# Half of a decode layer's result leaves through ScalarE, with its residual added in PSUM, and one store in place of two

## The chip, the cores and the metric

The kernel runs on one core of a Trainium2 chip. The metric is device time in microseconds (us) from start to end of one execution; lower is better. Of the kernel before, three runs are known: 189.81, 189.96 and 190.07 us, median 189.96. Engines are named as in the profile: PE (TensorE, matrix products), PEld (its weight loads), DVE (VectorE), ACT (ScalarE), POOL (GpSimd), SP (SyncE, which here only issues transfers and waits).

## What is computed

One token (a row `x` of 512 numbers) goes through an attention block with a cached context, and then through a small mixer and MLP block:

```python
def _A_ref(x, k_cache, v_cache, wq, wo):      # 32 query heads, 8 key/value heads, 16384 keys of 128
    q = (x @ wq) per head
    p = softmax(q k^T * 128**-0.5)
    return (p v over all heads) @ wo
def _B_ref(x, w1, w2, w3, w4):
    h  = gelu(layernorm(x) @ w1)
    hs = shifted quarters of h @ w2           # a shift over a sequence of one: all zero
    x1 = x + hs                               # so x1 = x, and w1, w2 are not needed
    return x1 + gelu(layernorm(x1) @ w3) @ w4
h  = x + _A_ref(layernorm(x), ...)
h2 = h + _B_ref(layernorm(h), ...)            # 512 bfloat16 numbers: the result
```

The caches are 2 x 32 MB of bfloat16, so nearly all bytes are keys and values. The result is the sum of a residual (`h` plus its normalised self, since `_B_ref` adds its input) and the product with `w4`.

## The kernel before, in words

**Stages.** The query projection comes first, then a loop over 4 pairs of key/value heads, and then a tail: the product with `wo`, the layer norm, the product with `w3`, gelu, the product with `w4`, the addition of the residual, the store. All large loads are issued by SP on one queue, in the order in which they are used: `wq`, keys, values, ..., `wo` (2 pieces), `w3`, `w4` (3 pieces, cut at groups 8 and 13 of 14, `W4`).

**How the code is recorded.** A helper class `Program` records operations with the keys that they read (`r`), write (`w`) and the PSUM banks that they use (`bank`). `op` (line 50) turns these into waits. For a bank it makes an operation wait for the last user of that bank on every other engine (lines 66 to 69), whatever part of the bank either touches. `_tensor` (line 159) folds PE's part of the loop over the pairs into a real loop on the engine, with registers: `r` ("seen") holds the DVE count to wait for, `rl` ("landed") the count of a POOL semaphore that tells which pair's values have landed. POOL's operation there is a `nop` that waits for the transfer and raises the semaphore by `worth`, which is 1.

**The tail as far as the change touches it.** `h_ps` is PSUM bank 6. The row of 512 is kept as 4 blocks of 128 columns; block `o` stands on partitions 32o to 32o+31, every one of them the same. `hT` and `hr` hold `h`; `st[1]` (`s`) holds its statistics, a column for each: `s[:, 6:7]` is an inverse root that POOL works out (`inverse_root(1, 0, pool, pool)`, line 787), `s[:, 13:14]` that plus one (line 788). ACT makes `xsum`, the residual on all 128 partitions, from `xs`, a per-partition scale `s[:, 13:14]` and a per-partition bias `s[:, 12:13]` (line 799). Gelu runs in two halves on ACT (line 791), each turned over by DVE into `hcol` (line 795). The product with `w4` (line 805) has 14 groups (`m`) of 4 matmuls (`o`), each with weights `hcol[:, m, :]` and 128 columns of `w4`; the groups from 7 on need the second half of `hcol`, those from 8 on the second piece of `w4`, group 13 the third. DVE adds `h_ps` and `xsum` into `fin` (line 810). Partitions 31 and 32 of `fin` hold blocks 0 and 1, partitions 95 and 96 blocks 2 and 3; SP stores the first two rows and ACT the other two (line 817), and SP waits for both (line 820).

Of the kernel before, what the change touches and what calls it, by code (L numbers as in the profile page):

```python
# [24 lines left out]
class Program:  # L25
# [133 lines left out]
    def _tensor(self):  # L159
        nc, eng, ops = self.nc, self.nc.tensor, self.ops["PE"]  # L160
        inside = [n for n, o in enumerate(ops) if o.at is not None]
        lo, hi = inside[0], inside[-1] + 1
        at = {o.at: o for o in ops[lo:hi]}
        assert len(at) == len(inside) == hi - lo
        loop = [o for o in ops[lo:hi] if o.at[0] != "query"]
        pairs = 1 + max(o.at[1] for o in loop)
        last = pairs - 1

        def places(kind, *rest):
            return sorted(a for a in at if a[0] == kind and a[1:1 + len(rest)] == rest)  # L170
# [3 lines left out]
        def least(o):  # L174
            return max((d.val - d.worth + 1 for d in o.deps if d.eng == "DVE" and not d.dma), default=0)
# [6 lines left out]
        parts = 1 + max(a[2] for a in places("value", last))  # L182
        step = least(at[("key", 2, 0, 0, 0)]) - least(at[("key", 1, 0, 0, 0)])
# [7 lines left out]
        first = waits["key", last, 0, 0, 0] - 1  # L191
        keys = {("key", last, y, c, 0): first + 1 + pieces * y + c for y in range(2) for c in range(pieces)}
        rest = {(a[0], a[-1]): v for a, v in waits.items() if a[0] in ("middle", "rest")}
# [5 lines left out]
        for o in loop:  # L199
            a = o.at  # L200
            v = waits.get((a[0], last, *a[2:]))
# [6 lines left out]
        told = {}  # L208
# [4 lines left out]
            for d in ds:  # L213
                told.setdefault(o.at[1:3], set()).add((d.sem, d.val - d.worth + 1, d.val))
        told = {k: max(v, key=lambda x: x[2]) for k, v in told.items()}
        sem, v0, _ = told[0, 0]
        for (j, x), (_, lo_v, hi_v) in told.items():
            assert lo_v <= v0 + parts * j + x <= hi_v
        assert v0 > 0 and first - step * last > 0

        r, rl, ry, rq, rk = (eng.alloc_register(n) for n in ("seen", "landed", "half", "query", "piece"))
        hint = eng.mark_branch_hint_location()
        eng.reg_mov(r, first + 1 - step * last)
        eng.reg_mov(rl, v0 - 1)
        seen = {}
        self._run(eng, ops[:lo], seen)
        query = [at[a] for a in places("query", 0)]
# [51 lines left out]

        nc.switch_bb("pe_middle", parent=None)  # L280
        now, again = first + 1 + 2 * pieces, 0
        eng.reg_add(rl, rl, 1)

        def straight(kind):
            nonlocal now, again
# [18 lines left out]
                nc.switch_bb(f"pe_ready{again}", parent=None)  # L304

        straight("middle")
        for x in range(parts):
            if x:
                eng.reg_add(rl, rl, 1)
            eng.wait_ge(sem, rl)  # L310
            for a in places("value", 1, x):
                self._issue(eng, at[a])
        straight("rest")
        assert now == final
        eng.reg_add(r, r, first + 1 - (final - step))
        eng.reg_add(ry, ry, -2 * 512 - again)
        eng.br_lt(rl, v0 - 1 + parts * pairs, "pe_piece", "pe_after")

        nc.switch_bb("pe_after", parent=None)
        seen[id(vector)] = final  # L320
# [16 lines left out]
            done = more + ops[more].many  # L337
        self._run(eng, ops[done:on], seen)

        eng.br_lt(rl, 0, "pe_piece", "pe_on").branch_hint(hint)  # L340
        nc.switch_bb("pe_on", parent=None)
        self._run(eng, ops[on + 1:], seen)

# [10 lines left out]
NHC = FM // 128  # L354
WO = ((0, 20), (20, 32))
VP = 1
W3 = ((0, 4),)
W4 = ((0, 8), (8, 13), (13, 14))
PAIRS = HKV // 2
# [12 lines left out]
def bass_sequential_preLN__gqa_block_cached__mixer_s_mlp__decode_kernel(  # L372
# [13 lines left out]
    with ExitStack() as ctx:  # L386
        sb = lambda name, shape, dt: ctx.enter_context(nc.sbuf_tensor(name, shape, dt))
        ps = lambda name, shape, dt: ctx.enter_context(nc.psum_tensor(name, shape, dt))
        P = Program(nc, ctx)
# [33 lines left out]
        bias = sb("bias", [128, 1], FP32)  # L423
# [11 lines left out]
        rs = [sb(f"rs{i}", [128, 2], FP32) for i in range(2)]  # L435
        hc = sb("hc", [128, NCH, 32], BF16)
        xs = sb("xs", [128, 128], FP32)
        xsum = sb("xsum", [128, 128], FP32)
        hg = sb("hg", [128, FQ], BF16)
        hT = sb("hT", [128, NCH, 32], FP32)  # L440
        hcol = sb("hcol", [128, NHC, 32], BF16)
        fin = sb("fin", [128, 128], BF16)
        kb_all = sb("kb", [128, 256 * DH], BF16)
        kb = [kb_all[:, i * 128 * DH:(i + 1) * 128 * DH] for i in range(2)]
        vb = sb("vb", [128, 256 * DH], BF16)
# [24 lines left out]
        def load_values(j):  # L470
            n = 256 // VP * DH
            if j < PAIRS - 1:
                load("v", vb[:, :], pair_rows(A_v_cache, j), ("v", 0),
                     also=[("v", x) for x in range(1, VP)] + [("landed", x) for x in range(VP)])
                P.op("POOL", lambda e: e.nop(), r=[("v", 0)], w=[("landed", x) for x in range(VP)], worth=VP,
                     own="v")
                return
            for x in range(VP):
                load(f"v{x}", vb[:, x * n:(x + 1) * n], pair_rows(A_v_cache, j)[:, x * n:(x + 1) * n], ("v", x),
                     also=[("landed", x)])  # L480
            for x in range(VP):
                P.op("POOL", lambda e: e.nop(), r=[("v", x)], w=[("landed", x)], own="v")  # L482


        def dve(fn, r=(), w=(), bank=()):
            return P.op("DVE", fn, r, w, bank)

        def act(fn, r=(), w=(), bank=()):
            return P.op("ACT", fn, r, w, bank)
# [57 lines left out]
        def inverse_root(i, n, by, beside):  # L547
# [9 lines left out]
            for m in range(3):  # L557
# [8 lines left out]
        load("x4", x4[:, :], A_x[0, 0:1, :].rearrange("o (q j) -> (o q) j", q=4), "x4", "ACT")  # L566
        load("wq", wq_sb[:, 0:NCH * HQ * DH], A_wq.rearrange("(p k) c -> p (k c)", k=NCH), ("v", 0), also=[("v", x) for x in range(1, VP)])
        load_keys(0, 0)
# [10 lines left out]
            r=["ident_f", "x4"], w=["quarter"])  # L579
        pe(lambda e: e.matmul(O_ps[0][:, 0:128], quarter[:, :, :].rearrange("p q u -> p (q u)"), x4[:, :],  # L580
                              start=True, stop=True), r=["quarter"], w=[("O", 0)], bank=[("O", 0)])
# [9 lines left out]
            r=["ident_f"], w=["row32"])  # L591
        dve(lambda e: e.tensor_reduce(maskdd[:, :], ident_f[:, :].rearrange("p (n d) -> p d n", d=4), AX.X, ALU.add),
            r=["ident_f"], w=["maskdd"])
# [3 lines left out]
        for z, src, key, of, n in ((zo, row32[:, :].rearrange("p (g n h) -> p g h n", g=2, h=REP), "zo", "row32", 4),  # L597
# [6 lines left out]
            r=["hT", (("st", 0), 0), (("st", 0), 6)] + [("v", x) for x in range(VP)], w=["xn"])  # L604
# [156 lines left out]
        h_ps, hkey = banks[:, 6, :], "spare0"  # L761
        for n in range(2):
            dve(lambda e, n=n: e.tensor_copy(osum[:, 256 * n:256 * n + 256], O_ps[0][:, 256 * n:256 * n + 256]),
                r=[("O", 0)], w=[("osum", n)], bank=[("O", 0)])
        for q in range(4):
            pe(lambda e, q=q: e.matmul(h_ps[32 * q:32 * q + 32, 0:128], copies(row32[:, 0:1], 32),
                                       osum[:, q * 128:(q + 1) * 128], start=True, stop=True),
               r=[("osum", q // 2), "row32"], w=[hkey], bank=[hkey])
        s = st[1]
        S = ("st", 1)  # L770
        row_sums(1, h_ps, hkey)
        act(lambda e: e.activation(hc[:, :, :], hT[:, :, :], ACTF.Identity, bias=s[:, 0:1], scale=1.0),
            r=["hT", (S, 0)] + [("r", 1, 0)], w=["hc"])
# [3 lines left out]
        for k in range(NCH):  # L777
            for q in range(4):
                pe(lambda e, k=k, q=q: e.matmul(s_ps[32 * q:32 * q + 32, 0, 0:FQ], hc[:, k, :],
                                                w3_sb[:, k, q * FQ:(q + 1) * FQ], start=(k == 0), stop=(k == NCH - 1)),  # L780
                   r=["hc"] + [("r", 1, n) for n in (piece(W3, k),) if n], w=[("s", 0)], bank=[("s", 0)])
        act(lambda e: e.activation(s[:, 12:13], s[:, 0:1], ACTF.Identity, scale=-1.0), r=[(S, 0)], w=[(S, 12)])
# [6 lines left out]
        for n in range(2):  # L789
            lo, hi = n * NHC // 2, (n + 1) * NHC // 2  # L790
# [5 lines left out]
                hcol[:, lo:hi, :].rearrange("p m u -> p (m u)"),  # L796
                hg[:, :].rearrange("p (i m) -> p m i", m=NHC)[:, lo:hi, :]), r=[("hg", n)] + [("r", 1, len(W3))] * (n == 0), w=[("hcol", n)])

        act(lambda e: e.activation(xsum[:, :], xs[:, :], ACTF.Identity, bias=s[:, 12:13], scale=s[:, 13:14]),
            r=["xs", (S, 12), (S, 13)], w=["xsum"])  # L800
        for m in range(NHC):
            if m == 4:
                pe(None)
            for o in range(4):
                pe(lambda e, m=m, o=o: e.matmul(  # L805
                    h_ps[32 * o:32 * o + 32, 0:128], hcol[:, m, :], w4_sb[:, m, o * 128:(o + 1) * 128],
                    start=(m == 0), stop=(m == NHC - 1), skip_group_check=True),
                   r=[("hcol", 2 * m // NHC)] + [("r", 1, len(W3) + n) for n in (piece(W4, m),) if n],
                   w=[hkey], bank=[hkey])
        dve(lambda e: e.tensor_tensor(fin[:, :], h_ps[:, 0:128], xsum[:, :], ALU.add), r=[hkey, "xsum"], w=["fin"],  # L810
            bank=[hkey])
        dve(None)


        for n, by in enumerate(("SP", "ACT")):
            lo = 64 * n + 31
            P.op(by, lambda e, n=n, lo=lo: e.dma_start(
                out[0, 0:1, 256 * n:256 * n + 256].rearrange("o (q j) -> (o q) j", q=2), fin[lo:lo + 2, :]),
                r=["fin"], w=[("out", n)], dma=f"out{n}")
        P.op("SP", lambda e: e.nop(), r=[("out", 0), ("out", 1)])  # L820
        P.emit()

    return nc
# [28 lines left out]
```

## Time and profile before

| what | value |
|---|---|
| median of three runs | 189.96 us (189.81 to 190.07) |
| the profiled execution, its own time | 189.9 us |
| its span, first to last instruction | 188.5 us |
| PE busy, of the span | 130.8 us, 69% |
| DVE busy | 116.6 us, 62% |
| ACT busy | 14.1 us, 7% |
| POOL busy | 6.9 us, 4% |
| read from HBM | 79.17 MB, 420 GB/s over the span |
| mean granted TensorE clock | 0.919 of full |

Times in the trace count from the start of the span. The profiled execution takes 1.4 us more than its span, and lies 0.06 us under the median, so it may be used as a stand-in for the three runs. The busy shares are averages over stages with quite different limits. The change lies almost wholly in the last 3 us, where hardly anything overlaps, so the timeline of those 3 us tells more than the shares.

### The profile page before, as it was taken

How to read it: one execution, taken by the hardware profiler on the slowest of the kernel's cores; microseconds unless marked ns; L12 is line 12 of the kernel's file. 1: busy time of each engine (PE TensorE's matmuls, PEld its weight loads, DVE VectorE, ACT ScalarE, POOL GpSimd, SP SyncE). 2: the span in 40 equal slices, each digit the busy share in tenths (PEclk: the TensorE clock that was granted, in tenths of full speed). 3: DMA queues.
4: the chain of work that ended last, by engine and by line, in shares of the span. 5: the costliest groups of instructions: out<-in, count | busy, mean ns of one | idle time of the engine just before them, and what ended most of it. 6: DMA issues, size and time to landing. Idle time of an engine off the chain costs nothing.

```text
span 188.5 us, 2414 instructions
## 1 busy us (share of the span) xinstructions
PE 130.8 (69%) x766; PEld 50.4 (27%) x767; DVE 116.6 (62%) x136; ACT 14.1 (7%) x23; POOL 6.9 (4%) x16
## 2 busy tenths in 40 slices
PE   0109903979789329797992297979929998795873
PEld 0103301323225113232250133322503333232321
DVE  5740599698251696982516969725169996534063
ACT  3000200000040000000400000004000000500012
POOL 8100000000000000000000000000000000000012
PEclk9999975699999957999999579999996999999699
DMA  6999999999799999979999999997999998989994
GB/s 223 445 445 445 445 445 445 445 445 445 334 445 445 445 556 417 389 306 445 445 445 445 445 445 445 445 445 334 445 445 445 556 445 389 403 349 411 422 415 173
DMA packets 2753, 79.19 MB, mean 420 GB/s; under 512 B 320, under 2 KB 448, under 8 KB 576
## 3 DMA queue, kind: packets, MB, share of 16 engines
q1 hardware_dynamic: 2740, 79.17, 97.8%
q8 instruction: 1, 0.02, 0.0%
q10 hardware_dynamic: 12, 0.00, 0.0%
HBM read 79.17 MB, written 0.00 MB: 420 GB/s over the span
## 4 chain that ended last, share of the span: by engine, by line
PE 43%; DVE 28%; DMA 23%; issue 5%; ACT 0%; DVEq 0%; SPq 0%; POOLq 0%; ACTq 0%
DVE kt L634 19%; DMA vb<-in_A_v_cache_dram 16%; PE banks L645 16%; PE banks L500 9%; PE banks L685 8%; DMA vb<-in_A_wq_dram 6%; PE banks L611 5%; PE banks L754 2%; DVE mx L659 2%; DVE od L704 2%; PE banks L662 1%; DVE qcol L618 1%; PE banks L707 1%; PE banks L805 1%; DVE od L701 1%
## 5 line engine op out<-in xcount | busy, mean ns | idle before, releaser
L645 PE MATMUL banks<-kt,qn 128*128 x256 | 69.6, 415 | 25.7 <-DVE kt L634 25.6
L634 DVE STREAM_TRANSPOSE kt<-kb 128x4096 int32<-128x4096 int32 (+2 forms) x25 | 70.6, 2878 | 4.8 <-PE banks L645 4.8
L645 PEld LDWEIGHTS banks<-kt,qn 128*128 x256 | 26.2, 102 | 68.5 <-issue 52.9
L500 PE MATMUL banks<-qb 128*128 128x512 bf16 x69 | 25.3, 388 | 0.8 <-issue 0.2
L685 PE MATMUL banks<-vb,pt 128*32 128x512 bf16 x256 | 14.7, 379 | 0.2 <-POOLq L482 0.2
L670 ACT ACTIVATE p_sb<-banks,bias 128x1024 bf16<-128x1024 f32 x4 | 4.5, 1114 | 132.4 <-DVE nmh L666 132.4
L611 PE MATMUL banks<-vb,xn 128*128 x32 | 9.6, 472 | 6.7 <-DVE xn L602 6.7
L659 DVE TENSOR_REDUCE mx<-banks 128x1 f32<-128x1024 f32 x4 | 4.9, 1224 | 14.6 <-PE banks L645 14.6
L674 DVE STREAM_TRANSPOSE pt<-p_sb 64x1024 bf16<-64x1024 bf16 x8 | 9.9, 1240 | 5.4 <-ACT p_sb L670 5.3
L500 PEld LDWEIGHTS banks<-qb 128*128 128x128 bf16 x70 | 6.7, 97 | 18.7 <-issue 18.4
L701 DVE TENSOR_SCALAR od<-banks,rowc 128x128 f32<-128x128 f32 x4 | 1.4, 351 | 13.8 <-PE banks L685 13.8
L685 PEld LDWEIGHTS banks<-vb,pt 128*32 128x32 bf16 x256 | 8.5, 97 | 4.5 <-POOLq L482 0.3
L618 DVE STREAM_TRANSPOSE qcol<-banks 64x1024 f32<-64x1024 f32 x4 | 4.8, 1228 | 7.8 <-PE banks L611 7.8
L611 PEld LDWEIGHTS banks<-vb,xn 128*128 128x128 bf16 x32 | 3.7, 116 | 12.1 <-issue 10.0
L556 POOL TENSOR_SCALAR st<-st 128x1 f32<-128x1 f32 x1 | 0.2, 247 | 177.3 <-DVE st L536 177.3
L662 PE MATMUL banks<-mxd,mean 128*128 128x128 f32 x8 | 2.0, 326 | 6.6 <-DVE mxd L660 6.6
L707 PE MATMUL banks<-od,zo 128*32 128x128 f32 x8 | 1.6, 285 | 6.5 <-DVE od L704 6.5
L654 ACT ACTIVATE banks<-mean 128x1024 f32<-128x1024 f32 x4 | 4.1, 1027 | 19.6 <-DVE qcol L618 19.5
L754 PE MATMUL banks<-kb,o_b 128*32 128x512 bf16 x44 | 4.6, 560 | 1.1 <-DVE o_b L750 1.1
L694 DVE RECIPROCAL den<-banks 32x1 f32<-32x1 f32 x4 | 0.6, 155 | 7.0 <-PE banks L692 7.0
L704 DVE SCALAR_TENSOR_TENSOR od<-banks,rowc,od 128x128 f32<-128x128 f32 x12 | 4.2, 351 | 0.4
L580 PE MATMUL banks<-x,quarter 4*128 4x128 bf16 x1 | 0.3, 283 | 5.4 <-DVE quarter L578 5.4
(75 smaller groups left out, 46.0 us busy)
## 6 DMA issues: line engine op xcount, KB each, us to landing
kb<-in_A_k_cache_dram SPq DMA_DIRECT2D x8, 4096.0 KB, 26.2
vb<-in_A_wq_dram SPq DMA_DIRECT2D x1, 4096.0 KB, 12.2
kb<-in_A_wo_dram SPq DMA_DIRECT2D x1, 2560.0 KB, 25.0
kb<-in_B_w_dram SPq DMA_DIRECT2D x1, 1792.0 KB, 23.9
kb<-in_A_wo_dram SPq DMA_DIRECT2D x1, 1536.0 KB, 28.3
kb<-in_B_w_dram SPq DMA_DIRECT2D x1, 1024.0 KB, 26.0
kb<-in_B_w_dram SPq DMA_DIRECT2D x1, 640.0 KB, 27.2
kb<-in_B_w_dram SPq DMA_DIRECT2D x1, 128.0 KB, 27.0
```

The source lines that it names most:

```text
L500: P.op("PE", lambda e: e.matmul(O_ps[1][:, :], field[:, 0:128], field[:, 0:512], start=True, stop=True), r=["qb"], bank=[("O", 1)], times= ...
L611: pe(lambda e, k=k: e.matmul(row[:, bass.ds(P.b + P.b0, 512)], copies(xn[:, k:k + 1], 128), wq_k[:, k, bass.ds(P.c + P.c0, REP * DH)], sta ...
L618: dve(lambda e, g=g, b=b, half=half: e.transpose(qcol[64 * g:64 * g + 64, 2 * b:2 * b + 2, :, :].rearrange("p e m u -> p (e m u)"), half.r ...
L634: P.op("DVE", lambda e, view=view: e.transpose(view(kt), view(kb[y])), r=[("r", y, i) for i in range(RPARTS)], w=[("kt", t + i) for i in r ...
L645: pe(lambda e, n=n: e.matmul(row[:, bass.ds(P.y, 512)], qn[:, n, bass.ds(P.q, 128)], key_piece(P.k, n), start=False, stop=(n == 3), skip_g ...
L654: act(lambda e: e.activation(s_all, copies(mean4[:, 0:1], 1024), ACTF.Identity, scale=0.0), r=["mean4", "p"], w=[("s", 0), ("s", 1)], **both)
L659: dve(lambda e: e.tensor_reduce(mx[:, :], s_all, AX.X, ALU.max), r=[("s", 0), ("s", 1)], w=["mx"], **both)
L670: act(lambda e: e.activation(p_sb[:, :], s_all, ACTF.Exp, bias=bias[:, 0:1], scale=float(SCALE), accum_out=acc[:, :]), r=[("s", 0), ("s", ...
L674: dve(lambda e, g=g: e.transpose(pt[64 * g:64 * g + 64, :, :, g, :], p_sb[64 * g:64 * g + 64, :]), r=["p"], w=["pt"])
L685: pe(lambda e, l=l, ct=ct, ch=ch: e.matmul(O_ps[0][32 * ct:32 * ct + 32, :], pt[:, l, ch, :, :].rearrange("p g u -> p (g u)"), tiles[:, l ...
L704: dve(lambda e, block=block, c=c: e.scalar_tensor_tensor(od[:, :], block, rowc[:, c:c + 1], od[:, :], ALU.mult, ALU.add), r=[key, "rowc", ...
L754: pe(lambda e, r_=r_, q=q: e.matmul(O_ps[0][32 * q:32 * q + 32, :], copies(o_b[:, r_:r_ + 1], 32), wo_sb[:, r_ * D:(r_ + 1) * D], start=(r ...
```

## The change

The residual of the upper two blocks (partitions 64 to 127) is written by ACT into `h_ps` itself, ahead of the product with `w4`; the matmuls of those blocks start with `start=False`, so that they add to what lies there. The residual of the lower two blocks stays in `xsum`, now 64 partitions, made by a second ACT operation. After the product DVE adds the lower half into columns 0 to 127 of `fin` as before, on 64 partitions; ACT copies the upper half from `h_ps` into columns 128 to 255. `fin` is now 64 x 256, and its rows 31 and 32 hold all four blocks, two in each row. SP stores them with one transfer of 2 x 2 x 128; ACT's store is gone. The dependency rules of `op` are unchanged.

In the loop on PE the register `rl` is gone. The POOL `nop` now raises its semaphore by 47 (`SEEN`) the first time and by 28 (`ROUND`) after that, so that its count can be waited for with the register `r`, whose value at that point grows by 28 from pair to pair.

```diff
+        held = max(v for (kind, n), v in rest.items() if kind == "middle")
...
-        eng.reg_mov(rl, v0 - 1)
...
         now, again = first + 1 + 2 * pieces, 0
-        eng.reg_add(rl, rl, 1)
...
-        for x in range(parts):
-            if x:
-                eng.reg_add(rl, rl, 1)
-            eng.wait_ge(sem, rl)
-            for a in places("value", 1, x):
-                self._issue(eng, at[a])
+        assert parts == 1 and now == held
+        eng.wait_ge(sem, r)
+        for a in places("value", 1, 0):
+            self._issue(eng, at[a])
...
-        eng.br_lt(rl, v0 - 1 + parts * pairs, "pe_piece", "pe_after")
+        eng.br_lt(r, first + 2, "pe_piece", "pe_after")
...
-                P.op("POOL", lambda e: e.nop(), r=[("v", 0)], w=[("landed", x) for x in range(VP)], worth=VP,
-                     own="v")
+                P.op("POOL", lambda e: e.nop(), r=[("v", 0)], w=[("landed", x) for x in range(VP)],
+                     worth=ROUND if j else SEEN, own="v")
...
-        act(lambda e: e.activation(xsum[:, :], xs[:, :], ACTF.Identity, bias=s[:, 12:13], scale=s[:, 13:14]),
-            r=["xs", (S, 12), (S, 13)], w=["xsum"])
+        act(lambda e: e.activation(h_ps[64:128, 0:128], xs[64:128, :], ACTF.Identity, bias=s[64:128, 12:13],
+                                   scale=s[64:128, 13:14]), r=["xs", (S, 12), (S, 13)], w=[hkey], bank=[hkey])
+        act(lambda e: e.activation(xsum[:, :], xs[0:64, :], ACTF.Identity, bias=s[0:64, 12:13],
+                                   scale=s[0:64, 13:14]), r=["xs", (S, 12), (S, 13)], w=["xsum"])
         for m in range(NHC):
...
-                    start=(m == 0), stop=(m == NHC - 1), skip_group_check=True),
+                    start=(m == 0 and o < 2), stop=(m == NHC - 1), skip_group_check=True),
                    r=[("hcol", 2 * m // NHC)] + [("r", 1, len(W3) + n) for n in (piece(W4, m),) if n],
                    w=[hkey], bank=[hkey])
-        dve(lambda e: e.tensor_tensor(fin[:, :], h_ps[:, 0:128], xsum[:, :], ALU.add), r=[hkey, "xsum"], w=["fin"],
+        dve(lambda e: e.tensor_tensor(fin[:, 0:128], h_ps[0:64, 0:128], xsum[:, :], ALU.add), r=[hkey, "xsum"],
+            w=[("fin", 0)], bank=[hkey])
+        act(lambda e: e.activation(fin[:, 128:256], h_ps[64:128, 0:128], ACTF.Identity), r=[hkey], w=[("fin", 1)],
             bank=[hkey])
         dve(None)
-        for n, by in enumerate(("SP", "ACT")):
-            lo = 64 * n + 31
-            P.op(by, lambda e, n=n, lo=lo: e.dma_start(
-                out[0, 0:1, 256 * n:256 * n + 256].rearrange("o (q j) -> (o q) j", q=2), fin[lo:lo + 2, :]),
-                r=["fin"], w=[("out", n)], dma=f"out{n}")
-        P.op("SP", lambda e: e.nop(), r=[("out", 0), ("out", 1)])
+        P.op("SP", lambda e: e.dma_start(out[0, 0:1, :].rearrange("o (h q j) -> (o q) h j", h=2, q=2),
+                                         fin[31:33, :].rearrange("p (h j) -> p h j", h=2)),
+             r=[("fin", 0), ("fin", 1)], w=["out"], dma="out")
+        P.op("SP", lambda e: e.nop(), r=["out"])
```

More of the change, by code (lines that the diff above doesn't have):

```diff
@@ L215, in _tensor @@
         told = {k: max(v, key=lambda x: x[2]) for k, v in told.items()}
-        sem, v0, _ = told[0, 0]
+        sem, _, _ = told[0, 0]
+        held = max(v for (kind, n), v in rest.items() if kind == "middle")
         for (j, x), (_, lo_v, hi_v) in told.items():
-            assert lo_v <= v0 + parts * j + x <= hi_v
-        assert v0 > 0 and first - step * last > 0
-        r, rl, ry, rq, rk = (eng.alloc_register(n) for n in ("seen", "landed", "half", "query", "piece"))
+            assert x == 0 and lo_v <= held + step * (j - last) <= hi_v
+        assert first - step * last > 0
+        r, ry, rq, rk = (eng.alloc_register(n) for n in ("seen", "half", "query", "piece"))
         hint = eng.mark_branch_hint_location()
         eng.reg_mov(r, first + 1 - step * last)
-        eng.reg_mov(rl, v0 - 1)
         seen = {}
@@ L338, in _tensor @@
         self._run(eng, ops[done:on], seen)
-        eng.br_lt(rl, 0, "pe_piece", "pe_on").branch_hint(hint)
+        eng.br_lt(r, 0, "pe_piece", "pe_on").branch_hint(hint)
         nc.switch_bb("pe_on", parent=None)
@@ L356 @@
 VP = 1
+SEEN, ROUND = 47, 28
 W3 = ((0, 4),)
@@ L437, in bass_sequential_preLN__gqa_block_cached__mixer_s_mlp__decode_kernel @@
         xs = sb("xs", [128, 128], FP32)
-        xsum = sb("xsum", [128, 128], FP32)
+        xsum = sb("xsum", [64, 128], FP32)
         hg = sb("hg", [128, FQ], BF16)
@@ L441, in bass_sequential_preLN__gqa_block_cached__mixer_s_mlp__decode_kernel @@
         hcol = sb("hcol", [128, NHC, 32], BF16)
-        fin = sb("fin", [128, 128], BF16)
+        fin = sb("fin", [64, 256], BF16)
         kb_all = sb("kb", [128, 256 * DH], BF16)
@@ L481, in load_values @@
             for x in range(VP):
-                P.op("POOL", lambda e: e.nop(), r=[("v", x)], w=[("landed", x)], own="v")
+                P.op("POOL", lambda e: e.nop(), r=[("v", x)], w=[("landed", x)], worth=ROUND, own="v")
         def dve(fn, r=(), w=(), bank=()):
```

## The prediction

> **What bounds the kernel now.** I read the chain of work that ended last first, to see which stage the change touches and what precedes it. Its last entries (start, length in us, engine, what):
>
> ```profile
> 137.61 30.46 DMA vb<-in_A_v_cache_dram
> 168.17 3.67 PE banks L685 x61
> ...
> 184.44 0.50 ACT hg L791
> 184.96 0.59 DVE hcol L795
> 185.60 1.26 PE banks L805 x56
> ```
>
> The last pair's values land at 168.17. From there to the end one step hands over to the next: gelu on ACT, a transposition on DVE, the product with `w4` on PE. So what the tail loses or gains from 184 us on reaches the end whole, unless a load is later. I then read the timeline of the last 4 us (start, length, engine, what, and in brackets the idle time before and who ended it), because the chain shows neither the residual nor the stores:
>
> ```profile
> 184.19 0.16 DVE L562 SCALAR_TENSOR_TENSOR st<-st,sti 128x1 f32<-128x1 f32 x1
> 184.44 0.85 ACT L791 ACTIVATE hg<-banks,st 128x224 bf16<-128x224 f32 x2 [1.33 <-DVE st L562]
> 184.96 1.05 DVE L795 STREAM_TRANSPOSE hcol<-hg 128x224 bf16<-128x224 bf16 x2 [0.62 <-ACT hg L791]
> 185.39 0.23 POOL L788 TENSOR_SCALAR st<-st 128x1 f32<-128x1 f32 x1
> 185.60 1.23 PE L805 MATMUL banks<-kb,hcol 128*32 128x128 bf16 x56 [1.58 <-DVE hcol L795]
> 185.71 0.49 ACT L799 ACTIVATE xsum<-xs,st 128x128 f32<-128x128 f32 x1 [0.41 <-POOL st L788]
> 186.88 0.29 DVE L810 TENSOR_TENSOR fin<-banks,xsum 128x128 bf16<-128x128 f32 x1 [0.87 <-PE banks L805]
> 187.20 0.33 SPq L817 DMA_DIRECT2D out_dram<-fin  x1
> 187.20 0.26 ACTq L817 DMA_DIRECT2D out_dram<-fin  x1
> ```
>
> The reader is to see three things. PE starts at 185.60, while the residual is only begun at 185.71, since POOL's column ends at 185.62; today that costs nothing, as `xsum` is ready at 186.20 and wanted at 186.88. Both stores are issued at the same moment, 187.20. And nothing runs beside DVE's addition. The span ends 1.33 us after the stores' issue (188.53).
>
> Then PE alone between 185.55 and 185.95, to have the pace of the product without its waits, and the table by stretches (columns: length, busy time of PE, PEld, DVE, ACT, POOL with counts, granted clock, DMA share, GB/s) for the load that comes last:
>
> ```profile
> 185.60 0.57 PE L805 MATMUL banks<-kb,hcol 128*32 128x128 bf16 x27 [1.58 <-DVE hcol L795]
> ```
>
> ```profile
> 186.00:186.10 0.10, 0.10 (x17) 0.04 (x4) 0.01 (x1) 0.10 (x1) 0.00 (x0) 1.00 0.13 41
> 186.10:186.20 0.10, 0.10 (x12) 0.07 (x4) 0.00 (x0) 0.10 (x1) 0.00 (x0) 1.00 0.00 0
> 187.90:188.00 0.10, 0.00 (x0) 0.00 (x0) 0.00 (x0) 0.00 (x0) 0.00 (x0) 1.00 0.06 10
> ```
>
> Seven groups of four matmuls take 0.57 us, a matmul 0.22, so groups follow each other by (0.57 - 0.22) / 6 = 0.058 us. Fourteen without a wait would take 13 x 0.058 + 0.22 = 0.97; they take 1.23, so 0.26 us of waiting lies inside, for `hcol`'s second half (ends 186.02) and for `w4` (its last data move at about 186.1). The clock is granted whole. The data of both stores move in one and the same tenth of a microsecond.
>
> Last the groups by line and form, for ACT's prices (line, engine, operation, count, busy, mean ns of one, idle before):
>
> ```profile
> L654 ACT ACTIVATE banks<-mean 128x1024 f32<-128x1024 f32 x4 | 4.1, 1027 | 19.6 <-DVE qcol L618 19.5
> L791 ACT ACTIVATE hg<-banks,st 128x224 bf16<-128x224 f32 x2 | 0.9, 489 | 1.3 <-DVE st L562 1.3
> L799 ACT ACTIVATE xsum<-xs,st 128x128 f32<-128x128 f32 x1 | 0.5, 493 | 0.4 <-POOL st L788 0.4
> L783 ACT ACTIVATE xs<-hr,st 128x128 f32<-128x128 f32 x1 | 0.4, 386 | 0.0
> L782 ACT ACTIVATE st<-st 128x1 f32<-128x1 f32 x1 | 0.2, 186 | 0.0
> ```
>
> **The change, step by step.**
>
> *The residual ahead of the product.* The ACT write into `h_ps` takes the place of line 799 in ACT's queue and waits for the same POOL column, so it starts at 185.71. Every matmul of the product writes that bank, so the very first waits for it, and all 56 stand behind that one. Price: 0.49, line 799's own (two per-partition operands, 128 elements). It differs in 64 partitions and in PSUM as destination; the nearest rows give 0.39 (line 783, one such operand) from below and, with the 0.02 that line 791 pays for reading PSUM (worked out below), 0.51 from above. It ends at 186.20. Handover to PE: 0.04 at least (`hcol`'s second half ends 186.02, PE loads at 186.06), 0.16 at most (DVE's `kt` ends 31.35, the chain has PE at 31.51); I take 0.09, what POOL to ACT takes here (185.62 to 185.71), as both wait for two semaphores. PE starts at 186.29 instead of 185.60. By then `hcol` and `w4` are there, so the waits inside vanish: it ends at 186.29 + 0.97 = 187.26 instead of 186.83. Of 0.69 us of later start 0.43 is left.
>
> *The lower residual.* A second ACT operation of 0.49 ends by 186.70; DVE wants it at 187.31. 0.6 us of slack, cost nothing; uncovered it would be 0.49.
>
> *DVE's addition.* 0.05 after PE's end as now, and 0.29 still: halving partitions does not shorten an operation here (line 709 on 32 partitions 0.34, line 704 on 128 partitions 0.35, with as many elements on each). From 187.31 to 187.60.
>
> *ACT's copy of the upper half.* It uses the same bank as DVE's addition and is recorded behind it, so by the helper's rule it waits for that addition to end. The two do not run beside each other. Handover 0.09 (DVE's column ends 184.35, ACT starts 184.44, also two semaphores). Its price: one element without per-partition operands takes 0.186 (line 782), 1024 take 1.027 (line 654), so 0.82 ns each, 128 give 0.29. Line 791 would by this be 0.186 + 0.10 for its one operand + 223 x 0.82 = 0.47 and takes 0.49, so PSUM as source adds 0.02: 0.31. Ends: 0.29 to 0.49 (line 799). ACT runs from 187.69 to 188.00.
>
> [...]
>
> *The store.* SP issues when both halves are there: 0.03 after DVE now, 0.09 at most as in the other waits for two semaphores; I take 0.06, so 188.06 instead of 187.20. One store of four pieces costs what the SP store of two costs now, 0.33 to issue and 1.33 to the end of the span. The lower end is -0.07 (ACT issued its store in 0.26; the two may have hindered each other), the upper +0.23 (the first load, of four pieces, took 0.56 to issue). I take 0, since the loads of 128 rows also issue in 0.33. Dropping ACT's store gains nothing, as it ran beside SP's and moved its data in the same tenth.
>
> *The loop on PE.* A register move and an addition for each pair go, the wait is for the same landing; POOL's `nop`s are as many as before. PE and SP each gain one waiting instruction, counted above. In each round the removed addition stood where PE waits for DVE's maximum (1.24 us), and from 137.61 on the transfer of the values sets the pace anyway. Cost nothing. Uncovered it would be small: a round of PE's idle loop, with an addition and a branch, takes 0.39 to 0.43 against its matmul's 0.38, so some 0.05, at most 0.2 us over four pairs, as a gain.
>
> *Sum.* 0.43 (PE) + 0.09 + 0.31 (copy behind the addition) + 0.03 (SP) = 0.86 us. On the profiled execution's 189.9 us this gives 190.76; that execution lies 0.06 under the median, so 190.8 us.
>
> **The rivals.** *The halves overlap after all* (the waits would have to be other than I read them). PE's delay stays; the copy ends at 187.26 + 0.09 + 0.31 = 187.66, the store goes at 187.72, 0.52 later than now: 190.5. Against it stands the rule for banks in `op`. *The load hides the late start.* If `w4` in the timed runs lands 0.4 us later against the rest than in the profile, today's PE also ends later, and only 0.43 is left: 190.4. The three runs lie within 0.26 us, which speaks against so large a shift. *The four pieces cost* 0.23 more to issue: 191.0. For it speaks the first load alone, which was also ACT's first. *The other side: one store is cheaper than two.* If the end were held up by the second store's completion, the 1.33 us after the issue would shrink; from 0.48 us saved it is no change, from 0.86 a gain, and with all of 0.86 saved the time would be 189.96. Against it: both stores' data move within 0.1 us, so the second can hold up the end by no more than that.
>
> **How the numbers follow.** A measurement of this kernel can tell about 0.2%, 0.38 us. Chances: my forecast 0.66, overlap 0.07, hidden start 0.07, dear pieces 0.13, cheap store 0.07. The forecast's own range is 190.6 to 191.0 (the handovers and the copy's 0.29 to 0.49). The range down to 190.4 and up to 191.1 takes in all but the cheap store and loses little more. Slower by over 0.2%: the forecast, the overlap and the dear pieces, 0.86, and most of the hidden start: 0.91. The cheap store is split, 0.06 same (with the rest of the hidden start) and 0.03 faster.
>
> **What would show it.** The first matmul of the product starts behind ACT's write, near 186.3, and its idle time is ended by ACT and no longer by DVE; the 56 matmuls take about 0.97. ACT's copy starts about 0.09 after DVE's addition ends, with the wait put down to DVE. There is one store, near 188.06, and the span ends 1.33 behind it at 189.4. I am wrong if the copy begins with the addition, if PE starts before 186.1, or if the stretch from store to end changes by more than 0.2.

## The result, and the profile after

The changed kernel took 190.55 us (median of 18 runs, 190.02 to 191.31), the kernel before beside it 189.96 (18 runs, 189.75 to 190.36). The ratio is 1.0033, 95% interval 1.0019 to 1.0046: slower by a third of a percent. The spread has grown with the median. Nine of the 18 runs lie at 190.02 to 190.37 (called the lower group below), two at 190.73 and 190.77, seven at 191.03 to 191.31 (the upper group); those seven are the only ones with a mean granted TensorE clock under 0.915 (0.908 to 0.914, the others 0.917 to 0.933).

The profiled execution took 190.73 us, with a span of 189.42. Its timeline from POOL's column on (start, length, engine, line, what; in brackets the idle time before and who ended it):

```profile
185.61 0.23 POOL L787 TENSOR_SCALAR st<-st 128x1 f32<-128x1 f32 x1
185.93 0.46 ACT L799 ACTIVATE banks<-xs,st 64x128 f32<-64x128 f32 x1 [0.41 <-POOL st L787]
186.41 0.49 ACT L801 ACTIVATE xsum<-xs,st 64x128 f32<-64x128 f32 x1
...
186.53 0.96 PE L807 MATMUL banks<-kb,hcol 128*32 128x128 bf16 x56 [2.32 <-ACT banks L799]
187.54 0.28 DVE L814 TENSOR_TENSOR fin<-banks,xsum 64x128 bf16<-64x128 f32 x1 [1.31 <-PE banks L807]
187.92 0.27 ACT L816 ACTIVATE fin<-banks 64x128 bf16<-64x128 f32 x1 [1.01 <-DVE fin L814]
188.26 0.32 SPq L819 DMA_DIRECT2D out_dram<-fin  x1
```

PE's wait ahead of the product is now ended by ACT's write and is 2.32 us long, where it was 1.58 and ended by DVE. The 56 matmuls run in 0.96 without a wait inside. ACT's copy begins 0.10 after DVE's addition has ended. The chain of work that ended last (start, length, what) has gelu and the transposition no longer in it; in their place stand POOL's operations up to the column, too short to be listed here, and ACT's write:

```profile
185.93 0.46 ACT banks L799
186.53 0.99 PE banks L807 x56
```

From the end of POOL's column to the end of the span, the kernel before took 188.53 - 185.62 = 2.91 us, this one 189.42 - 185.84 = 3.58: 0.67 more. The other 0.22 us of the longer span came earlier, POOL's column being that much later in this execution.

### The profile page after: what moved, and what is told of

The parts are those of the page before. It is cut to its first block, busy times and chain, and to the rows that moved or that the text cites. A ratio compares the mean times of both kernels' runs of the same rounds, so it can differ in the third digit from the quotient of the medians.

```text
span 189.4 us, 2417 instructions
## 1 busy us (share of the span) xinstructions
PE 130.0 (69%) x766; PEld 50.4 (27%) x767; DVE 116.7 (62%) x136; ACT 14.9 (8%) x25; POOL 6.9 (4%) x16
## 4 chain that ended last, share of the span: by engine, by line
PE 42%; DVE 27%; DMA 23%; issue 5%; POOL 1%; ACT 0%; DVEq 0%; ACTq 0%; SPq 0%; POOLq 0%
DVE kt L633 19%; DMA vb<-in_A_v_cache_dram 16%; PE banks L644 15%; PE banks L499 9%; PE banks L684 8%; DMA vb<-in_A_wq_dram 6%; PE banks L610 5%; DVE mx L658 2%; DVE od L703 2%; PE banks L753 2%; PE banks L661 1%; DVE qcol L617 1%; PE banks L706 1%; DVE od L700 1%; POOL st L559 1%
## 5 line engine op out<-in xcount | busy, mean ns | idle before, releaser
L684 PE MATMUL banks<-vb,pt 128*32 128x512 bf16 x256 | 16.4, 411 | 0.9 <-POOLq L481 0.9
L684 PEld LDWEIGHTS banks<-vb,pt 128*32 128x32 bf16 x256 | 9.0, 103 | 6.3 <-issue 2.2
L555 POOL TENSOR_SCALAR st<-st 128x1 f32<-128x1 f32 x1 | 0.2, 247 | 177.6 <-DVE st L535 177.6
L753 PE MATMUL banks<-kb,o_b 128*32 128x512 bf16 x44 | 3.1, 383 | 1.1 <-DVE o_b L749 1.1
```

Source lines behind the costliest of these rows:

```text
L684: pe(lambda e, l=l, ct=ct, ch=ch: e.matmul(O_ps[0][32 * ct:32 * ct + 32, :], pt[:, l, ch, :, :].rearrange("p g u -> p (g u)"), tiles[:, l ...
```

## The experiments

Each ratio is to runs of the kernel before on the same chip, beside the variant, with a 95% interval.

**The loop alone, and the tail alone.** The first has the kernel before with the edit of PE's loop (`rl` folded into `r`, `worth` 47 and 28), the second the changed kernel without it:

```diff
-            eng.wait_ge(sem, rl)        # loop_only: this and the lines around it, as in the change
+            eng.wait_ge(sem, r)
...
-            eng.wait_ge(sem, r)         # tail_only: the same lines taken back
+            eng.wait_ge(sem, rl)
```

> The kernel before with the change's edit of PE's loop alone: the register rl folded into r, POOL's nop raising its semaphore by 47 and 28. Nothing of the tail is changed. The changed kernel's runs spread from 190.0 to 191.3 us, those of before from 189.8 to 190.4, and this run asks whether the loop makes that spread. Theory 1 (the loop edit is neutral, all of the change's cost and its spread come from the tail): 190.0 us within 0.2, runs between 189.7 and 190.4. Theory 2 (the loop edit shifts PE's work against the clock's pattern): some 190.3 to 190.6, with runs up to 191.

> The changed kernel with the loop of before (rl kept, POOL's nop raising by 1): the tail's edit alone. Theory 1: as the changed kernel, 190.4 to 190.8 us, with its spread up to 191.3. Theory 2 (the loop makes the spread): 190.2 to 190.3 and no run over 190.6.

The loop alone: 190.01 us, 189.72 to 190.15, ratio 1.0004 (0.9995 to 1.0012). It is neutral. The tail alone: 190.99 us in six runs, 190.14 to 191.48, ratio 1.0057 (1.0038 to 1.0076). So cost and spread both come from the tail; with six runs in so wide a spread the median itself says little. The profile of the tail alone shows an execution at 190.20 us, and in it something that the first profile did not show:

```profile
184.70 0.23 POOL L790 TENSOR_SCALAR st<-st 128x1 f32<-128x1 f32 x1
185.02 0.46 ACT L802 ACTIVATE banks<-xs,st 64x128 f32<-64x128 f32 x1 [0.24 <-POOL st L790]
...
185.62 0.63 PE L810 MATMUL banks<-kb,hcol 128*32 128x128 bf16 x32 [1.85 <-ACT banks L802]
...
186.45 0.52 PE L810 MATMUL banks<-kb,hcol 128*32 128x128 bf16 x24 [0.20 <-DMA kb<-in_B_w_dram]
```

POOL's column ends at 184.93 here, 0.9 us sooner than above. PE still starts behind ACT's write, but after 32 matmuls (eight groups) it waits for the second piece of `w4`. The product ends at 186.97, little later than in the kernel before (186.83).

**The copy beside the addition.** ACT's copy is no longer recorded as a user of the bank:

```diff
-        act(lambda e: e.activation(fin[:, 128:256], h_ps[64:128, 0:128], ACTF.Identity), r=[hkey], w=[("fin", 1)],
-            bank=[hkey])
+        act(lambda e: e.activation(fin[:, 128:256], h_ps[64:128, 0:128], ACTF.Identity), r=[hkey], w=[("fin", 1)])
```

> The changed kernel, with ACT's copy of the upper half no longer recorded as a user of the bank, so that it waits for PE alone and may run beside DVE's addition. Theory 1 (the copy stands behind the addition only by the helper's rule): the copy starts about 0.10 us after PE's end and takes 0.27 to 0.31, the store is issued 0.44 to 0.50 after PE's end instead of 0.77, and the time falls by about 0.3 us against the changed kernel, to some 0.3 over before. Rival (the two readers of one bank slow each other): the copy or the addition takes over 0.4, and less than 0.1 is won.

Median 189.83 us in 12 runs, ratio 1.0007 (0.9991 to 1.0023): nine runs at 189.63 to 190.05, as fast as the kernel before, and three at 190.82 to 191.40. The profiled execution is one of the three:

```profile
186.18 1.68 PE L807 MATMUL banks<-kb,hcol 128*32 128x128 bf16 x56 [2.32 <-ACT banks L799]
187.91 0.28 ACT L816 ACTIVATE fin<-banks 64x128 bf16<-64x128 f32 x1 [1.35 <-PE banks L807]
187.91 0.28 DVE L814 TENSOR_TENSOR fin<-banks,xsum 64x128 bf16<-64x128 f32 x1 [2.03 <-PE banks L807]
188.26 0.32 SPq L818 DMA_DIRECT2D out_dram<-fin  x1
```

Both halves start together and take 0.28 us each, no longer than one after the other (0.28 and 0.27 in the changed kernel), so the copy stood behind the addition only by the helper's rule. The store is issued 0.40 us after PE's end, where it was 0.77.

The other thing to see is 1.68 us for the product. The table by stretches, PE alone (length, busy time with count, granted clock, DMA share, GB/s):

```profile
185.00:186.00 1.00, 0.00 (x0) 0.88 0.73 270
186.00:187.00 1.00, 0.82 (x33) 0.50 0.01 4
187.00:188.00 1.00, 0.87 (x35) 0.50 0.06 16
```

The clock falls to half within PE's idle stretch (0.88 over the microsecond from 185.0 puts the fall at about 185.8), and the whole product runs at half speed.

**The residual early.** The upper half's residual is scaled by another column, which is ready early, and written ahead of gelu. The upper half of the result is then another; the operation is of the same form:

```diff
-        act(lambda e: e.activation(h_ps[64:128, 0:128], xs[64:128, :], ACTF.Identity, bias=s[64:128, 12:13],
-                                   scale=s[64:128, 13:14]), r=["xs", (S, 12), (S, 13)], w=[hkey], bank=[hkey])
...
+        act(lambda e: e.activation(h_ps[64:128, 0:128], xs[64:128, :], ACTF.Identity, bias=s[64:128, 12:13],
+                                   scale=s[64:128, 12:13]), r=["xs", (S, 12)], w=[hkey], bank=[hkey])   # ahead of line 786
```

> The changed kernel with the residual of the upper half scaled by a column that is ready early (minus the mean in place of one plus the inverse root), and written ahead of gelu; the upper half of the result is not the reference's. Theory 1 (PE waits for ACT's write, which waits for POOL's column): PE starts when hcol's first half is there, as before, and the time falls by 0.3 to 0.5 us against the changed kernel. Rival (the late start is absorbed by w4's landing, and the change costs by its last copy alone): under 0.15 us is won.

190.21 us, 190.06 to 190.56 in 11 runs, ratio 1.0019 (1.0010 to 1.0027). The upper group is gone, and the runs lie within 0.5 us:

```profile
183.22 0.46 ACT L786 ACTIVATE banks<-xs,st 64x128 f32<-64x128 f32 x1
...
185.76 1.12 PE L807 MATMUL banks<-kb,hcol 128*32 128x128 bf16 x56 [1.62 <-DVE hcol L796]
```

PE starts with `hcol` again. What stays, about 0.3 us, is ACT's copy behind the addition, less what the single store gives back.

**Matmuls that nobody reads, in PE's idle stretch.** Four, and then seven, between the products with `w3` and `w4` of the changed kernel, with the changed kernel itself again beside the seven:

```diff
+        for n in range(4):              # warm; range(7) in warm7
+            unread(None)
         for m in range(NHC):
```

> The changed kernel with four matmuls that nobody reads put on PE between the product with w3 and the product with w4, where PE only waits; everything else as changed. The changed kernel's runs fall into two groups, some 190.0 to 190.4 and 190.7 to 191.3; the upper one was seen in the three kernels in which PE waits for ACT's write, and not in those in which it doesn't; in the profile of the run with the halves beside each other the clock drops to half at 185.8 us and the product takes 1.68 us instead of 0.96. Theory 1 (the longer idle stretch of PE ahead of the product, 2.3 us instead of 1.6, lets the clock fall in part of the executions): with four matmuls of about 0.4 us in that stretch the upper group is gone, all runs 190.0 to 190.5. Rival (the upper group has to do with the write into PSUM itself or with where the code lies): the upper group stays.

> The changed kernel once more, on the same chip and in the same call as the next one, to be compared with it run by run: time against mean granted clock. In its first 18 runs 7 had a mean clock of 0.914 or less, and they took 191.0 to 191.3; the four-matmul variant had none so low in 12. Theory 1 (a half-clock stretch falls into the product with w4 in part of the executions): again a group over 190.9 with a clock of at most 0.914, in a quarter to a half of the runs. Rival (that group was an accident of one chip): none here.

> The changed kernel with seven matmuls that nobody reads between the products with w3 and w4, where four were tried: some 1.7 us of work, so that PE's idle stretch ahead of the product shrinks from about 2.3 to about 0.7 us. Theory 1: no run with a mean clock of 0.914 or less, none over 190.95; the runs from 190.0 to 190.9 stay, since the late start and ACT's copy stay. Rival (the low clock has nothing to do with PE's idle stretch): as many slow runs as in the changed kernel beside it.

With four: 190.35 us, 190.04 to 190.91 in 12 runs, ratio 1.0023 (1.0014 to 1.0031), no clock under 0.917. The rows of the profile, an execution at 190.91:

```profile
184.21 1.04 PE L499 MATMUL banks<-qb 128*128 128x512 bf16 x4
...
185.69 0.23 POOL L787 TENSOR_SCALAR st<-st 128x1 f32<-128x1 f32 x1
...
186.61 0.96 PE L809 MATMUL banks<-kb,hcol 128*32 128x128 bf16 x56 [1.36 <-ACT banks L799]
```

The product runs at full clock (0.96 us, against 1.68 at half in `beside`). Five of the 12 runs lie above the 190.5 that the first theory set; none of them has a low clock. In the profiled one POOL's column came late (185.92). The changed kernel again: 190.11 us, ratio 1.0021 (1.0006 to 1.0037); nine runs at 189.90 to 190.16 and two, with clocks of 0.910 and 0.911, at 191.14 and 191.49, rather fewer than the expected quarter to half. Its profiled execution, at 190.11, has a chain that ends with the second piece of `w4` and names what bounds the lower group:

```profile
158.84 27.45 DMA kb<-in_B_w_dram
186.33 0.56 PE banks L807 x24
```

With seven: no clock under 0.917 in six runs, PE idle for 0.70 us ahead of the product, spans of 188.7 to 189.5. The times, 190.69 to 191.72, are no evidence for or against, because in this kernel alone 1.9 to 2.4 us lie outside the span, where all others have 1.25 to 1.5. The expectation on its times failed for that reason; what lies outside the span the trace does not show, so the cause stays open.

**One wait alone.** The kernel before, with the product waiting for `xsum`:

```diff
-                   r=[("hcol", 2 * m // NHC)] + [("r", 1, len(W3) + n) for n in (piece(W4, m),) if n],
+                   r=[("hcol", 2 * m // NHC), "xsum"] + [("r", 1, len(W3) + n) for n in (piece(W4, m),) if n],
```

> The kernel before with one wait added and nothing else: the product with w4 waits for xsum, which ACT ends when it would end the changed kernel's write into PSUM. Theory 1 (the wait of PE and its idle stretch make the upper group, and w4's landing hides the late start in the other runs): a group at 189.8 to 190.1, as the kernel before, and a second one 0.6 to 1.1 above in a quarter to a half of the runs. Rival (the late start costs its 0.4 us in every run): all runs near 190.3. Second rival (the PSUM write is to blame): all runs as before.

189.96 us, ratio 1.0006 (0.9996 to 1.0015): eight of 11 runs at 189.69 to 189.97, and three at 190.19, 190.42 and 190.59. The highest run of the kernel before is 190.19 too, so two runs lie clearly above it. So a late start of PE by itself is hidden in most executions and costs some 0.5 to 0.7 us in a few; it does not cost its 0.4 in each. The group with the low clock did not show in these 11 runs (lowest 0.918), and this part of the expectation is not borne out. The profiled execution is a hidden one. The profile puts PE's wait down to DVE, whose operation ended at 185.68; the added wait is for `xsum`, which ended at 185.64, and PE starts 0.14 behind it, the handover that the changed kernel has too:

```profile
185.15 0.49 ACT L799 ACTIVATE xsum<-xs,st 128x128 f32<-128x128 f32 x1 [0.41 <-POOL st L788]
...
185.78 0.97 PE L805 MATMUL banks<-kb,hcol 128*32 128x128 bf16 x56 [2.24 <-DVE hcol L795]
```

**The single store alone.** DVE adds both halves, one after the other, and one transfer stores them:

```diff
-        dve(lambda e: e.tensor_tensor(fin[:, :], h_ps[:, 0:128], xsum[:, :], ALU.add), r=[hkey, "xsum"], w=["fin"],
-            bank=[hkey])
+        for n in range(2):
+            dve(lambda e, n=n: e.tensor_tensor(fin[0:64, 128 * n:128 * n + 128], h_ps[64 * n:64 * n + 64, 0:128],
+                                               xsum[64 * n:64 * n + 64, :], ALU.add), r=[hkey, "xsum"],
+                w=[("fin", n)], bank=[hkey])
```

> The kernel before with the new store alone: DVE adds both halves, one after the other, on 64 partitions each, into the two halves of the 64 x 256 fin, and SP stores all with one transfer; no write of ACT into PSUM, no copy by ACT. Profiles so far have 1.33 us from the issue of two stores to the end and 1.16 from the issue of one. Theory 1 (one store ends 0.17 us sooner than two, and the late start and ACT's copy are the change's cost): DVE's second addition costs 0.2 to 0.3, the store gives back 0.17, together 0.0 to 0.15 us over before and no upper group. Rival (the shorter end is ACT's doing, not the single store's): 1.33 stays, 0.2 to 0.3 over before.

190.06 us, ratio 1.0005 (0.9996 to 1.0014), no upper group. Even this, without ACT's write and ACT's copy, only breaks even:

```profile
187.25 0.61 DVE L811 TENSOR_TENSOR fin<-banks,xsum 64x128 bf16<-64x128 f32 x2 [0.68 <-PE banks L805]
187.88 0.32 SPq L817 DMA_DIRECT2D out_dram<-fin  x1
```

Two additions take 0.61 us instead of 0.29; the span ends at 189.04, 1.16 after the issue.

**The lower blocks first.** The copy beside the addition, the keys of the two halves of the bank kept apart (`w` is `("h", 0)` and `("h", 1)`), and the first seven groups in another order, so that only the upper blocks wait for ACT's write:

```diff
...
-        for m in range(NHC):
...
-            for o in range(4):
...
+        half = NHC // 2
+        order = [(m, o) for lo in (0, 2) for m in range(half) for o in (lo, lo + 1)]
+        order += [(m, o) for m in range(half, NHC) for o in range(4)]
...
```

> The changed kernel with ACT's copy beside DVE's addition and with the matmuls of the first seven groups in another order: all of the lower two blocks first, which need no residual in PSUM, then the upper two; only the latter wait for ACT's write. Theory 1: PE starts when hcol's first half is there, works 0.4 us before it meets ACT's write, so that the idle stretch is as short as before and the late start is hidden by w4's landing; the copy and the addition run together; the single store gives back 0.17. All runs 189.6 to 190.0, no upper group, 0.0 to 0.2 us under before. Rival (two blocks at a time leave PE too slow, or the write still comes too late): 190.0 to 190.4.

190.04 us, ratio 1.0010 (1.0001 to 1.0019): six runs at 189.74 to 189.95, six at 190.13 to 190.57, two of the latter with clocks of 0.909 and 0.915. The expected gain didn't come. In the profiled execution the plan works, and `w4` bounds the end as ever (the rows of PE's weight loads and matmuls):

```profile
185.40 1.47 PE L809 MATMUL banks<-kb,hcol 128*32 128x128 bf16 x56 [1.73 <-DVE hcol L794]
...
186.31 0.42 PEld L809 LDWEIGHTS banks<-kb,hcol 128*32 128x32 bf16 x24 [0.28 <-DMA kb<-in_B_w_dram]
```

No version here beats the kernel before; `beside` and `halves_first` reach it in their better runs and lose that in the others.

**What the end of the span waits for.** The kernel before with both stores issued by SP, and with SP's store alone, so that the upper half of the result is not stored:

```diff
-        for n, by in enumerate(("SP", "ACT")):
+        for n, by in enumerate(("SP", "SP")):        # sp_both; ("SP",) in sp_one
```

> The kernel before with both stores issued by SP, one after the other, none by ACT. From the last data of the store to the end of the span two stores have taken 0.53 us and one store 0.36. Theory 1 (it is the waiting for two completions, whoever issues them): 0.5 stays, and the second issue comes 0.3 later, 190.2. Theory 2 (it is ACT's queue having had a store): it falls to 0.36 and the time is about 190.0, the second issue's 0.3 less 0.17.

> The kernel before with SP's store alone; the upper half of the result is not stored. Theory 1 (two completions against one) and theory 2 (ACT's queue) both: 0.36 from the store's last data to the end of the span, 1.16 from its issue, 0.17 us under before. Rival (the 2 x 2 x 128 form of the new store, or the later moment at which it comes, makes the shorter end): 0.53 and 1.33 stay, no gain.

Both by SP: 190.11 us, ratio 1.0016 (1.0007 to 1.0025). One alone: 189.66 us, ratio 0.9992 (0.9983 to 1.0001). The issue, and then the tenth of a microsecond in which the last data move (table by stretches: length, busy times of the engines, clock, DMA share, GB/s), of SP's two:

```profile
187.38 0.64 SPq L817 DMA_DIRECT2D out_dram<-fin  x2
```

```profile
188.50:188.60 0.10, 0.00 (x0) 0.00 (x0) 0.00 (x0) 0.00 (x0) 0.00 (x0) 0.50 0.02 3
```

and of the single one:

```profile
187.90:188.00 0.10, 0.00 (x0) 0.00 (x0) 0.00 (x0) 0.00 (x0) 0.00 (x0) 1.00 0.03 5
```

By the trace's records the last packet of a store ends 0.35 us before the span does in both, as in the changed kernel (0.36); with a store issued by ACT it is 0.53 (the kernel before) and 0.54 (the loop alone). So it is not the number of completions: two stores of SP end as quickly as one. It is that ACT issues one of them, and this costs 0.18 us at the end. Why is not shown. A second issue on SP costs more than that: from the first issue to the end of the span it is 188.87 - 187.38 = 1.49 us with two, 188.36 - 187.21 = 1.15 with one and 1.33 in the kernel before, so 0.34 are paid for the 0.18 gained.

## Why the prediction was right, and where it was not

The direction and the range held: 190.55 us lies between 190.4 and 191.1, though just below the 190.6 to 191.0 that I gave the forecast itself. The cost was 0.59 us, not 0.86, and in the second comparison 190.11, or 0.24, which lies below the whole range. So the sum of 0.86 us is not how that number comes about. Step by step:

- *ACT's write ahead of the product.* Right in its parts: 0.09 after POOL's column, 0.46 us (0.49 forecast), handover 0.14 (0.09), product 0.96 (0.97). From POOL's column on, PE's end came 187.49 - 185.84 = 1.65 us later, against 186.83 - 185.62 = 1.21 in the kernel before: 0.44, as forecast (0.43).
- *That these 0.43 reach the end in every execution.* This is the step that failed. I made the sum against one execution, in which POOL's column ended at 185.62, and took that moment as given. In the thirteen other profiles it ends between 184.83 and 186.17, while the second piece of `w4` lets PE go on at 186.3 to 186.5 whenever it waits for it. Eight groups take 8 x 0.058 = 0.46, so a start up to 186.29 - 0.46 = 185.83 costs nothing, and with 0.09 + 0.46 + 0.14 before it that means a column that ends by 185.14, as in five of the thirteen. This is the rival "the load hides the late start", to which I gave 7 in 100 and for which I looked in the wrong place: `w4` is not later, the rest is sooner. The lower group of the changed kernel, some 0.2 to 0.3 over before, is that case, as the two profiles with a column at 184.83 (`after_again`) and 184.93 (`tail_only`) show. What moves the column is, as far as these profiles show it, where the half clock lies some 6 to 11 us earlier. Counted from the mean clock over stretches of 2 us, it is half from 174.2 to 177.6 in `tail_only`, from 174.9 to 178.4 in `loop_only`, from 175.5 to 178.9 in `beside`, from 175.8 to 179.3 in the kernel before and from 176.1 to 179.6 in `residual_early`; the column ends at 184.93, 185.20, 185.49, 185.62 and 185.77, in the same order. In the kernel before, the product with `wo` lies there: it runs from 174.88 to 179.52, 4.64 us. In the first profile of the changed kernel the clock is half from 168.3 to 171.7 instead, and the product with the values takes 5.32 us where it took 3.64; the product with `wo` starts 1.69 us later, at 176.57, but takes 3.19 us at full clock, and the column ends 0.22 later.
- *ACT's copy behind the addition.* Right: 0.10 and 0.27 (0.09 and 0.31 forecast), by the helper's rule alone, as `beside` shows.
- *The store.* SP's issue came 0.07 after the copy (0.06 forecast). From issue to end it took 1.16 us and not 1.33: "dropping ACT's store gains nothing" was wrong by 0.17. That both stores' data move in the same tenth was rightly read, but it does not bound what a second store can cost, as I argued against the rival "one store is cheaper than two": the difference lies behind the data.
- *The lower residual and the loop.* Both cost nothing, as forecast: `xsum` ends at 186.90 and is wanted at 187.54, and the loop alone has the ratio 1.0004.
- *Left out:* the clock. I read that it was granted whole in the last stage and did not ask what a longer idle stretch would do to it. PE waits 1.58 us ahead of the product in the profile before and 2.32 in that after, and in 7 of 18 runs the mean clock was low, in all of which the time was 0.8 to 1.1 us above the lower group.

For the clock the evidence is this. Runs with a mean clock of at most 0.915: in the kernels in which PE waits for ACT (the changed one twice, `tail_only`, `beside`, `wait_xsum`) 15 of 58; in `loop_only`, `residual_early`, `one_store_dve`, `sp_both` and `sp_one` 1 of 53; in `halves_first`, where only the upper blocks wait, 2 of 12; in the kernel before, beside all these, 2 of 93; with four or seven idle matmuls 0 of 18. Of the 58, the 11 of `wait_xsum` have none. At the share of the other four kernels, 15 of 47, that would happen by chance about once or twice in 100 times. So the longer idle stretch by itself is not shown to bring the low clock, and a part of ACT's write into PSUM, the rival named ahead of these runs, is not excluded; against the write alone stand the 18 runs with idle matmuls and the 11 of `residual_early`, which have the write (the latter ahead of gelu) and no low clock.

Shown in a trace is the half clock in the product of `beside`, and of `sp_both`, whose product began at 185.26, took 1.75 us and ended only 0.2 later than usual; there the fall costs little, as PE would have waited for `w4` in between anyway. That the fall takes the seven runs of the changed kernel to 191 was seen by their clocks, not in a trace of one of them.

In `beside` the clock is half from 175.5 to 178.9, for 3.4 us, and falls again at 185.8, 6.9 us on. In the 3.4 us ahead of that fall (182.4 to 185.8) PE worked for 1.51 us, the last of it until 183.9.

In the profile of the kernel before, the clock is half for 10.24, 6.83, 6.83, 3.41 and 3.41 us (from 25.66, 66.62, 104.16, 141.71 and 175.84), and in the first of the changed kernel for 6.83, 6.83, 6.83, 3.41 and 3.41 (from 28.38, 65.92, 103.47, 141.01 and 168.32). These lengths, and those of the full clock between them, are multiples of 3.41 us. Where the half clock lies differs from execution to execution, and that fits a fall in only a part of them. How much work of PE goes with a kept clock is not shown. Counted back by steps of 3.41 us from a change of the clock, which is an estimate, the changed kernel keeps the full clock after a stretch with 2.23 us of PE's work (182.0 to 185.4, from the fall at 188.8), and the kernel before after one with 1.78 (182.7 to 186.1). `sp_both` loses it at 185.1; in the 3.41 us before that PE worked for at most 1.82, as it was idle from 183.53 on.

For the measured median: in the lower group PE's end is where it was, the copy and SP add 0.10 + 0.27 + 0.04, and the end gives back 0.17; that is 0.24, and the second comparison (0.24 between the medians) is just that. In the first comparison half of the runs lay above, with late columns or a low clock, and the median fell between the groups. A forecast of one number for such a distribution is met by chance as much as by its working.

## What to carry to other kernels

A delay that you read off one execution is added to the end only if nothing else is due there: before adding it, ask which load or semaphore the delayed engine would have met anyway, and in how many executions. A wait that lengthens an idle stretch of PE may have a second price, a half clock for what follows (behind 2.32 us of idling, 0.96 us became 1.68 in `beside`). A low clock came in some executions only (15 of 58 here), so look at the spread and at the clock of each run, not at the median alone. And a helper that orders engines by whole PSUM banks undoes a split of one evacuation over two engines, so read the waits that it makes of the new operations, not the intention.

## What the runs showed of the hardware that was not expected

- A store issued by ACT lengthens the end of the span by 0.18 us (last data to end 0.53 to 0.54 us with it, 0.35 to 0.36 without), whether SP issues one store or two.
- The granted clock fell to half within an idle stretch of PE of 2.32 us in `beside` and of 1.73 us in `sp_both`, and the next product then took 1.68 and 1.75 us, where it took 0.96 without a wait at full clock. Which executions it falls in is explained only in part.
- With nearly the same work ahead of it, POOL's column ended up to 1.3 us apart in the profiles (184.83 to 186.17). In five of them it ends the sooner (184.93 to 185.77), the sooner the stretch of half clock ahead of it begins (174.2 to 176.1).
- ACT's write of 64 x 128 numbers into PSUM took 0.46 us, its write of as many into SBUF, with the same two per-partition operands, 0.49.
- With seven idle matmuls more, 1.9 to 2.4 us lay outside the span, instead of 1.25 to 1.5; with four they did not. No cause was found.
